# Loading stored sums of w_out in the later batches instead of adding them again on VectorE

## The chip, the cores and the metric

The kernel runs on one core of one Trainium2 chip. The metric is the time of one execution on the device in microseconds (us); less is better. Below, PE or TensorE is the matmul engine, DVE or VectorE the vector engine, ACT or ScalarE the scalar engine, POOL or GpSimd the engine whose queue issues software DMAs, and SP the engine that here only issues DMAs.

## The reference

There are two parts in a row. The attention part has 4 batches, 8 heads, 768 positions and 64 columns a head. Each query and key gets a hash of 6 bits from the signs of its product with proj; scores between a query and a key of different hash are masked; softmax and the product with v follow. The result, reshaped to 3072 x 512, goes through an MLP:

```
h = x @ w_in                                   # 512 -> 2048
g = max(h, 0) + alpha * min(h, 0)
out = g @ w_out                                # 2048 -> 512
```

All is float32. The change is in the last product, g @ w_out. Since w_out is the same for all four batches, so is everything that is computed from w_out alone.

## The kernel before, in words

`fast_path` first runs the attention of all 16 pairs of heads (up to about 375 us), and rounds and regroups the weights on the way. The MLP follows, batch by batch (768 tokens each). Each batch has eight blocks of the first stage (`ff1`, called "1" in the list of blocks) and seven of the second (`ff2`, called "2").

Both stages use a Strassen-like scheme with seven products in place of eight, twice nested in the second stage. The outer seven products of the second stage are the seven blocks n = 0 to 6, in the order `ORDER = (1, 2, 5, 6, 3, 7, 4)`; in the profile they carry the names z_1, z_2, z_5, z_6, z_3, z_7 and z_4. For each, `load_w2` has SP load one tile of 1 MB, `wl`, with the outer combination of quarters of w_out (from w_out_r, or, where it is a sum, from w_out_s). It has two buffers, and is issued two blocks ahead. The nested product then needs four quarters of `wl` and four sums of them, the tiles ws3, ws4, ws5 and ws6 (256 KB each), which `sum_w2` computes on VectorE: 3 = 21 + 2, 4 = 3 − 0, 5 = 0 − 21, 6 = 1 − 4. ws3 and ws4 have two buffers, ws5 and ws6 one (`bufs=1 + (m < 5)`). The same four sums for g are computed by `sum_g2` (tiles gs3 to gs6).

A product is an object of `Product`, whose seven matmul groups are the steps 1, 2, 5, 6, 3, 7 and 4 (22 is VectorE's part of step 2). Step 1 multiplies the first quarter of `wl`, step 2 the second, step 4 the third; step 5 uses ws3, step 6 ws4, step 3 ws6, and step 7 ws5. The loop over blocks starts step 1 of the next product ahead of step 4 of the current one, so TensorE's order within a block is 2, 5, 6, 3, 7, next 1, 4. Step 4 is the last to read the current `wl`, and its buffer is then free for the load two blocks on.

The instructions wrapped in `do(...)` keep their program order on their engine; all computing instructions are. Of the DMAs only some are (through `pinned`). The others, `wl` among them, are placed on their queue by a planner, which takes the instruction of the highest priority (earliest in the program) that can start by its own costs; a tile's buffer is given on when everything that reads it is done. On a queue the order is then fixed.

In batches 1 to 3 the first stage is nested as well (`unit`, `Inner`). The tags ws3 to ws6 are lent there to other tiles of the same size: two tiles `wp` of `load_inner` take ws3 and ws4, and two intermediate results take ws5 and ws6. The sums of block 0 are made at the end of `unit(b, 1)`. Finished outputs are transposed on VectorE by `turn_out` and stored by DMAs of 32 KB, 12 for each of four parts, on SP's queue and partly on GpSimd's.

A sum over w_in in the same manner is already kept: `sum_inner` computes it in batch 1 and stores it to w_n_s, and batches 2 and 3 load it.

Of the kernel before, what the change touches and what calls it, by code (L numbers as in the profile page):

```python
# [8 lines left out]
F32 = mybir.dt.float32  # L9
# [398 lines left out]
def fast_path(  # L408
# [12 lines left out]
    nc = tc.nc  # L421
    P = 128
    B, H, S, D = q.shape
    NB = proj.shape[1]
    NTOK, DM = out.shape
# [17 lines left out]
    do = tc.keep_in_program_order  # L443
    PE, DVE, ACT, POOL = nc.tensor, nc.vector, nc.scalar, nc.gpsimd

    const = ctx.enter_context(tc.tile_pool(name="const", bufs=1))
    dram = ctx.enter_context(tc.tile_pool(name="dram", bufs=1, space=bass.MemoryType.DRAM))
# [24 lines left out]
    NI = NF // 2  # L472
# [2 lines left out]
    w_out_r = dram.tile([4, P, NI, DM // 2], F32, name="w_out_r")  # L475
    w_out_s = dram.tile([4, P, NI, DM // 2], F32, name="w_out_s")
    x_s = dram.tile([B, NP, P, S], F32, name="x_s")
    w_n_s = dram.tile([2, 2, P, 4, 2 * P], F32, name="w_n_s")
    NW = NK * NF // 2
    wmax = const.tile([P, NW], F32, name="wmax")  # L480
# [405 lines left out]
    def sum_x(b, n, engine):  # L886

        to, a, c = ((3, 5, 0), (5, 2, 5), (4, 2, 3), (6, 4, 1))[n]
        if to != 5:
            x_m[b, to] = mid.tile([P, 2, CW], F32, name=f"x{b}_{to}", tag=f"x{to}", bufs=1)  # L890
        do(engine.tensor_tensor(x_m[b, to], x_m[b, a], x_m[b, c], op=ALU.subtract))
# [154 lines left out]
    def sum_inner(b, u, o):  # L1046

        if b != 1:
            return
        for m, x, op, y in ((3, 21, ALU.add, 2), (4, 3, ALU.subtract, 0), (5, 0, ALU.subtract, 21), (6, 1, ALU.subtract, 4)):  # L1050
            do(DVE.tensor_tensor(n_w[b, u, o, m], n_w[b, u, o, x], n_w[b, u, o, y], op=op))
            nc.gpsimd.dma_start(w_n_s[u, o, :, m - 3].rearrange("p (t f) -> p t f", t=2), n_w[b, u, o, m])

    def sum_inner_x(b, o):

        x = x_m[b, 3 * o]
        if o == 0:
            t = mid.tile([P, 4, HC], F32, name=f"xn{b}_0", tag="x", bufs=1)
        else:
            t = late[0].tile([P, 4, HC], F32, name=f"xn{b}_1", tag="gs5", bufs=1)  # L1060
        left, right = (x[:, :, c * HC : (c + 1) * HC] for c in range(2))
        do(DVE.tensor_tensor(t[:, :2], right, x[:, 0].rearrange("p (c w) -> p c w", c=2), op=ALU.subtract))
        do(DVE.tensor_tensor(t[:, 2], right[:, 1], t[:, 0], op=ALU.subtract))
        do(DVE.tensor_tensor(t[:, 3], left[:, 1], t[:, 2], op=ALU.subtract))
        n_x[b, o] = {0: left[:, 0], 1: left[:, 1], 2: right[:, 1], 3: t[:, 0], 4: t[:, 2], 5: t[:, 1], 6: t[:, 3]}
# [68 lines left out]
    def unit(b, u, before):  # L1134
# [31 lines left out]
        if u:  # L1166
            sum_w2(b, 0, 3, 4, 6, 5)
# [12 lines left out]
    w2, g2, m2, to_turn = {}, {}, {}, []  # L1180
# [25 lines left out]
    def sides_g(b, n):  # L1206
        t = g_m[b, SIDES[ORDER[n]][1]]
        for m, kh, ch in ((0, 0, 0), (1, 1, 0), (2, 1, 1), (12, 0, 1)):
            g2[b, n, m] = t[:, kh * HK : (kh + 1) * HK, ch * HC : (ch + 1) * HC]

    def sum_w2(b, n, *ms):

        if n < 7:
            for m in ms:
                x, op, y = {
                    3: (21, ALU.add, 2), 4: (3, ALU.subtract, 0), 5: (0, ALU.subtract, 21), 6: (1, ALU.subtract, 4),
                }[m]
                w2[b, n, m] = t = late[0].tile([P, HK, H2], F32, name=f"ws{b}_{n}_{m}", tag=f"ws{m}", bufs=1 + (m < 5))
                do(DVE.tensor_tensor(t, w2[b, n, x], w2[b, n, y], op=op))  # L1219

    def sum_g2(b, n, *ms):

        if n < 7:
            for m in ms:
                x, y = {3: (12, 0), 4: (2, 3), 5: (2, 12), 6: (1, 4)}[m]
                g2[b, n, m] = t = late[0].tile([P, HK, HC], F32, name=f"gs{b}_{n}_{m}", tag=f"gs{m}", bufs=1 + (m < 5))
                do(DVE.tensor_tensor(t, g2[b, n, x], g2[b, n, y], op=ALU.subtract))  # L1227
# [95 lines left out]
    def largest():  # L1323
        do(DVE.memset(col, 0.0))
        do(DVE.tensor_reduce(top[:, :2], mags, axis=mybir.AxisListType.X, op=ALU.max))
        do(DVE.tensor_reduce(top[:, 2:3], wmax, axis=mybir.AxisListType.X, op=ALU.max))
        do(DVE.tensor_reduce(top[:, 3:4], alpha, axis=mybir.AxisListType.X, op=ALU.max))

    def verdict():
        ps = two_banks("vd")[:4, 0, :P]  # L1330
        do(PE.transpose(ps, top, ident))
        do(DVE.tensor_reduce(col[:4, 0:1], ps, axis=mybir.AxisListType.X, op=ALU.max))
        do(DVE.transpose(row, col))
        do(DVE.tensor_tensor(row[0:1, 0:1], row[0:1, 0:1], row[0:1, 1:2], op=ALU.mult))

        do(DVE.tensor_scalar(row[0:1, 0:1], row[0:1, 0:1], SAFE, None, op0=ALU.is_le))
        do(DVE.tensor_scalar(row[0:1, 2:3], row[0:1, 2:3], HI_END, None, op0=ALU.is_lt))
        do(DVE.tensor_scalar(row[0:1, 3:4], row[0:1, 3:4], 1.0, None, op0=ALU.is_le))
        do(DVE.tensor_tensor(row[0:1, 0:1], row[0:1, 0:1], row[0:1, 2:3], op=ALU.mult))
        do(DVE.tensor_tensor(row[0:1, 0:1], row[0:1, 0:1], row[0:1, 3:4], op=ALU.mult))  # L1340
        do(DVE.tensor_scalar(flag, row[0:1, 0:1], -1.0, 1.0, op0=ALU.mult, op1=ALU.add))
# [130 lines left out]
    for j, (b, what, n) in enumerate(blocks):  # L1472
        n2 = n + 1 if what == "2" else 0 if n == NI - 1 else 7
        if n2 == 0:
            sides_g(b, 0)
            if b == 0:
                sum_w2(b, 0, 3, 4)
        if not j:
            now.step(6)
        elif not (b and what == "1"):  # L1480
            now.step(2)
        if j == 0:
            now.step(3)
            now.step(7)
            now.step(2)
        if what == "2" and n == 6 and b + 1 < B:
            sum_inner(b + 1, 0, 0)
        now.step(22)
        if (b, what, n) == (1, "2", 1):
            largest()  # L1490
        if what == "2" and b + 1 < B and 2 <= n < 6:
            if n == 3:
                sum_inner_x(b + 1, 0)
            else:
                sum_x(b + 1, {2: 0, 4: 1, 5: 2}[n], DVE)
        if b and what == "1" and n == 1:
            load_inner(b, 1)
        if b and what == "1" and n in (2, 3):
            sum_inner(b, 1, n - 2)
        if 0 < n2 < 7:  # L1500
            sides_g(b, n2)
            sum_w2(b, n2, 3, 4)
        if n2 < 7:
            sum_g2(b, n2, 3, 4)
        if j:
            if not (b and what == "1"):
                now.step(5)
            now.step(6)
            now.step(3)
            if n2 or b == 0:  # L1510
                sum_w2(b, n2, 6)
            if b and what == "1" and (n + 1) % 4:
                after = ff1(b, n + 1)
                after.step(1)
            now.step(7)
            if n2 or b == 0:
                sum_w2(b, n2, 5)
            sum_g2(b, n2, 5)
        if (b, what, n) == (1, "2", 3):
            verdict()  # L1520

        for n_out in [(), (0,), (1,), (2, 3), (4,), (5, 6), (7,)][j] if j < 7 else ():
            sum_out(n_out)
        for n_out in [(1,), (2, 3), (4,), (5, 6), (7,)][j] if j < 5 else ():
            load_out(n_out)
        if what == "1":
            load_w(b * NI + n + 3)

            if b and n in (2, 5):
                load_w2(b, n // 4)  # L1530
            if not b and n >= NI - 2:
                load_w2(b, n - NI + 2)
        else:
            load_w2(b, n + 2)
            if b + 1 < B:
                if n == 5:
                    load_inner(b + 1, 0)
                if n == 0:
                    load_x(b + 1)
        if j + 1 == len(blocks):  # L1540
            turn_last(0)
        elif what == "1" or n < 6:
            turn_out()
        before = now
        if j + 1 < len(blocks):
            b1, what1, n1 = blocks[j + 1]
            if b1 and what1 == "1" and n1 % 4 == 0:
                now = unit(b1, n1 // 4, before)
            elif b1 and what1 == "1":
                now = after  # L1550
                now.step(2)
                now.step(5)
                before.step(4)
            else:
                now = ff1(b1, n1) if what1 == "1" else ff2(b1, n1)
                now.step(1)
                before.step(4)
        else:
            before.step(4)
        if n2 < 7:  # L1560
            sum_g2(b, n2, 6)
# [29 lines left out]
```

## Time and profile before

| what | value |
|---|---|
| median of 3 runs | 866.09 us (865.49 to 866.65) |
| profiled execution, its own time | 865.96 us |
| its span, first to last instruction | 863.8 us |
| granted TensorE clock, mean | 0.998 of full |
| TensorE matmul busy | 851.8 us |
| VectorE busy | 751.6 us |
| ScalarE busy | 415.9 us |
| GpSimd busy | 150.1 us |
| the four sums `ws` (L1219) on VectorE | 38.4 + 19.4 + 19.2 us, 112 instructions |
| DMA, over the span | 147.97 MB, 28.24 of them on GpSimd's queue |

A row of the profile names the line of the kernel (L1219), the engine, the operation, and then the tile written and those read (`ws<-wl`), with the number of instructions; buffer numbers are left out of the names. In a group's row follow the busy time in us, the mean of one in ns, and after the bar the idle time of the engine just before them and who ended it. In a timeline row the first number is the start in us from the start of the span, the second the duration; merged rows carry a count (x8), and the time in square brackets is the wait before, with its releaser. A row of the waits reads: the waiting engine, tile and line, the releaser, the sum in us, the number, the longest. PEld is TensorE's weight load, which runs ahead of its matmul, so the same wait shows there a little longer.

The second stage of the four batches lies at about 385 to 452, 520 to 587, 655 to 722 and 789 to 855 us.

### The profile page before, as it was taken

Reading aid. Unit: us, or ns where it says so; the run is one execution under the profiler, and the core shown is the slowest. Engines: PE = TensorE matmul, PEld = TensorE weight load, DVE = VectorE, ACT = ScalarE, POOL = GpSimd, SP = SyncE. Lnnn points to the kernel's source line nnn. Section 1 sums busy time; section 2 is a strip of 40 time slices with the busy share of each in tenths; the row PEclk is TensorE's granted clock in tenths of the full one; section 3 lists DMA queues with packets and bytes.
Section 4 is the critical chain, followed back from the end, with each engine's and each line's share of the span. In section 5 each row is a group of like instructions: output and inputs, shape, how many; then the busy total and the mean of one; then the engine's idle time right before and its main releaser. Section 6 shows DMA issues by size and latency. Waiting matters only on the chain.

```text
span 863.8 us, 15130 instructions
## 1 busy us (share of the span) xinstructions
PE 851.8 (99%) x5602; PEld 591.1 (68%) x5602; DVE 751.6 (87%) x1210; ACT 415.9 (48%) x778; POOL 150.1 (17%) x313
## 2 busy tenths in 40 slices
PE   9999999999999999999999999999999999999996
PEld 4444444444445445569996769998668999677996
DVE  6999999999999977889996979996769997769985
ACT  7777888878788833231115541114452114453111
POOL 1322423333334310210015100003000001200001
PEclk9999999999999999999999999999999999999999
DMA  8956879879698436775344734333845334830342
GB/s 203 191 130 132 205 178 240 167 205 243 131 252 208 145 126 234 245 288 215 128 141 139 276 134 170 120 144 97 315 140 174 143 109 130 297 135 0 104 159 60
DMA packets 174659, 147.97 MB, mean 171 GB/s; under 512 B 120832, under 2 KB 155824, under 8 KB 170992
## 3 DMA queue, kind: packets, MB, share of 16 engines
q1 hardware_dynamic: 159776, 117.35, 46.7%
q0 software_dynamic: 11792, 28.24, 10.8%
q10 hardware_dynamic: 3008, 1.33, 0.6%
q8 instruction: 46, 0.75, 0.4%
q14 instruction: 37, 0.30, 0.1%
HBM read 115.35 MB, written 30.41 MB: 169 GB/s over the span
## 4 chain that ended last, share of the span: by engine, by line


## 5 line engine op out<-in xcount | busy, mean ns | idle before, releaser
L790 ACT ACTIVATE pt<-sc 128x768 f32<-128x768 f32 x192 | 153.9, 813 | 3.1 <-PE sc L787 2.8
L787 PE MATMUL sc<-qT,kT 64*128 64x384 f32 x768 | 155.2, 482 | 0.0
L820 PE MATMUL av<-pt,vn 128*32 128x385 f32 (+1 forms) x1536 | 127.0, 485 | 0.0
L820 PEld LDWEIGHTS av<-pt,vn 128*32 128x32 f32 x1536 | 50.3, 109 | 73.8 <-issue 68.8
L787 PEld LDWEIGHTS sc<-qT,kT 64*128 64x128 f32 x768 | 68.9, 187 | 37.0 <-issue 36.9
L1281 POOL DMA_DIRECT2D out_dram<-o x52 | 28.3, 552 | 349.6 <-DVE o L1274 348.8
L983 DVE TENSOR_TENSOR g<-g,g 128x384 f32<-128x384 f32 (+1 forms) x92 | 63.5, 711 | 1.6
L787 PE MATMUL sc<-qb,kb 64*128 64x384 bf16 x384 | 63.9, 323 | 0.5 <-ACT pt L790 0.3
L979 DVE SCALAR_TENSOR_TENSOR g<-h,alpha 128x384 f32<-128x384 f32 x63 | 37.8, 612 | 20.7 <-ACT h L972 20.7
L1227 DVE TENSOR_TENSOR gs<-g,gs 128x768 f32<-128x768 f32 x56 | 53.2, 951 | 1.0
L1227 DVE TENSOR_TENSOR gs<-g 128x768 f32<-128x768 f32 x56 | 53.2, 950 | 0.0
L1219 DVE TENSOR_TENSOR ws<-wl 128x512 f32<-128x512 f32 x56 | 38.4, 685 | 11.3 <-DMA wl<-w_out_s 9.7
L787 PEld LDWEIGHTS <-kb 64*128 64x128 bf16 x384 | 20.2, 94 | 33.9 <-issue 11.6
L607 ACT ACTIVATE wr<-raw 128x512 int32<-128x512 uint32 x32 | 22.1, 692 | 30.3 <-DVE wso L651 15.3
L748 POOL DMA_DIRECT2D qb<-hr x60 | 30.0, 507 | 26.4 <-ACT hr L743 26.4
L798 DVE TENSOR_TENSOR accp<-pt,pt 128x1536 f32<-128x1536 f32 x16 | 28.1, 1756 | 7.3 <-ACT pt L790 7.3
L803 DVE TENSOR_TENSOR accd<-accd,pt 128x1536 f32<-128x1536 f32 x16 | 28.1, 1758 | 1.7
L809 DVE TENSOR_TENSOR accd<-accd,accp 128x1536 f32<-128x1536 f32 x16 | 28.1, 1758 | 0.6
L806 DVE TENSOR_TENSOR accp<-accp,pt 128x1536 f32<-128x1536 f32 x16 | 28.0, 1752 | 0.0
L802 DVE TENSOR_TENSOR accd<-pt,pt 128x1536 f32<-128x1536 f32 x16 | 28.0, 1751 | 0.0
L1431 ACT ACTIVATE qT<-qT 128x768 f32<-128x768 f32 x15 | 12.7, 844 | 25.4 <-DMA kb<-hr 20.8
L1239 DVE TENSOR_TENSOR m<-m,m 128x768 f32<-128x768 f32 x24 | 22.7, 946 | 0.3
(448 smaller groups left out, 1861.0 us busy)
## 6 DMA issues: line engine op xcount, KB each, us to landing
wi<-w_in_s SPq DMA_DIRECT2D x32, 896.0 KB
wl<-w_out_s SPq DMA_DIRECT2D x16, 1024.0 KB
wl<-w_out_r SPq DMA_DIRECT2D x12, 1024.0 KB
raw<-in_moe_w_in_dram POOLq DMA_DIRECT2D x15, 512.0 KB, 4.9
raw<-in_moe_w_out_dram POOLq DMA_DIRECT2D x14, 512.0 KB, 4.6
w_in_s<-wsi SPq DMA_DIRECT2D x16, 448.0 KB
qn<-in_q_dram SPq DMA_DIRECT2D x64, 96.0 KB
vn<-in_v_dram SPq DMA_DIRECT2D x16, 384.0 KB
```

What stands on the lines that cost most here:

```text
L748: queue.dma_start(bits[name, pi][D * s : D * s + 2 * NB, half * CW : (half + 1) * CW], raw[c : c + 2 * NB],)
L787: do(PE.matmul(sc[:, s, :CW], what["k", pi][r, ks], what["q", pi][r, qs], start=first, stop=not first,))
L790: do(ACT.activation(pts[kc][:, g, :, :CW], sc[:, :, :CW], AF.Exp, scale=SCALE / DOWN))
L798: do(DVE.tensor_tensor(accp[pi], p(0), p(1), op=ALU.add))
L803: do(DVE.tensor_tensor(accd[pi], accd[pi], p(5), op=ALU.add))
L809: do(DVE.tensor_tensor(accd[pi], accd[pi], accp[pi], op=ALU.add))
L820: do(PE.matmul(av[pi][D * s + t : D * s + t + 32, g, :w], nat["v", pi][:, s, kc * D + t : kc * D + t + 32], pts[kc][:, g, s, :w], start=(k ...
L979: do(DVE.scalar_tensor_tensor(new_g(b, m)[:, i], h, al, h, op0=ALU.mult, op1=ALU.max))
L983: do(DVE.tensor_tensor(new_g(b, to)[:, at], g_m[b, x][:, at], g_m[b, y][:, at], op=ALU.subtract))
L1219: do(DVE.tensor_tensor(t, w2[b, n, x], w2[b, n, y], op=op))
L1227: do(DVE.tensor_tensor(t, g2[b, n, x], g2[b, n, y], op=ALU.subtract))
L1281: pinned(b + 1 < B and queue is nc.sync, queue.dma_start(out_v[b, ch * CH + c].rearrange("(w r) d -> r w d", r=32)[:, :, cols], src[32 * a ...
```

## The change

A tensor w_f_s in device memory is added, with a place for each of the seven products and four sums. In batch 0 the sums are computed on VectorE as before, and each is also stored to w_f_s by a DMA on GpSimd's queue. In batches 1 to 3 `sum_w2` issues a load of 256 KB on GpSimd's queue into the same tile, and VectorE adds nothing. The order in which the sums appear in the program changes for these batches too: all four of the next product are asked for at once, in the order 3, 4, 6, 5, where the first two were before, and not spread over the block. Neither stores nor loads are pinned. Buffers, products and all other loads stay as they are.

```diff
+    w_f_s = dram.tile([7, 4, P, NI // 2, DM // 4], F32, name="w_f_s")
...
                 w2[b, n, m] = t = late[0].tile([P, HK, H2], F32, name=f"ws{b}_{n}_{m}", tag=f"ws{m}", bufs=1 + (m < 5))
-                do(DVE.tensor_tensor(t, w2[b, n, x], w2[b, n, y], op=op))
+                if b:
+                    nc.gpsimd.dma_start(t, w_f_s[n, m - 3])
+                else:
+                    do(DVE.tensor_tensor(t, w2[b, n, x], w2[b, n, y], op=op))
+                    nc.gpsimd.dma_start(w_f_s[n, m - 3], t)
...
         if 0 < n2 < 7:
             sides_g(b, n2)
-            sum_w2(b, n2, 3, 4)
+            sum_w2(b, n2, *((3, 4, 6, 5) if b else (3, 4)))
...
             now.step(3)
-            if n2 or b == 0:
+            if b == 0:
                 sum_w2(b, n2, 6)
...
             now.step(7)
-            if n2 or b == 0:
+            if b == 0:
                 sum_w2(b, n2, 5)
             sum_g2(b, n2, 5)
```

## The prediction

> **What bounds the kernel now.** I read the page's first section, then TensorE's timeline in the last batch, then TensorE's waits from 380 us on (the change acts only after that), then the SP queue with VectorE's waits, then DMA shares by stretch.
>
> ```profile
> span 863.8 us, 15130 instructions
> PE 851.8 (99%) x5602; PEld 591.1 (68%) x5602; DVE 751.6 (87%) x1210; ACT 415.9 (48%) x778; POOL 150.1 (17%) x313
> ```
>
> TensorE looks full and VectorE nearly so. Busy matmuls alone prove little, so I check the pace of the second MLP stage. A product is seven TensorE steps in the order 2, 5, 6, 3, 7, 1 of the next product, 4. The start times:
>
> ```profile
> 816.11 1.46 PE L921 MATMUL z_6a<-g,wl 128*128 128x192 f32 x8
> ...
> 826.02 1.58 PE L921 MATMUL z_3a<-g,wl 128*128 128x192 f32 x8 [0.64 <-DMA wl<-w_out_s]
> ...
> 835.23 1.46 PE L921 MATMUL z_7a<-g,wl 128*128 128x192 f32 x8
> ...
> 844.33 1.46 PE L921 MATMUL z_4a<-g,wl 128*128 128x192 f32 x8
> ```
>
> From 835.23 to 844.33 is 9.10 us: seven steps of 1.30 us, the pace at which steps follow each other without a wait. Only 816.11 to 826.02 is longer, 9.91 us, and its row names the releaser: a 1 MB load of wl. All waits of TensorE after 380 us:
>
> ```profile
> PE z_2c L921 <- DVE m L1248: 0.8, 1, 0.8
> PE z_3a L921 <- DMA wl<-w_out_s: 0.6, 1, 0.6
> PE nf L1084 <- DVE wp L1051: 0.4, 1, 0.4
> PE z_4c L921 <- DVE m L1248: 0.3, 1, 0.3
> PE z_7c L921 <- DVE m L1248: 0.2, 1, 0.2
> PE f_3c L921 <- ACT f_3c L999: 0.2, 1, 0.2
> ```
>
> That is 2.5 us in 480. VectorE ends only three of them in a second-stage product: z_2c (in the first batch, where the additions stay) and z_7c and z_4c of the second batch. So TensorE sets the time, and VectorE, though 87% busy, is nearly always in time.
>
> The next thing that could be late is wl. SP issues the third to fifth wl of the last batch, and VectorE's first additions wait for each landing:
>
> ```profile
> 800.66 18.57 SPq L1187 DMA_DIRECT2D wl<-w_out_s  x3
> 805.41 0.69 DVE L1219 TENSOR_TENSOR ws<-wl 128x512 f32<-128x512 f32 x1 [0.28 <-DMA wl<-w_out_s]
> 814.50 0.69 DVE L1219 TENSOR_TENSOR ws<-wl 128x512 f32<-128x512 f32 x1 [1.20 <-DMA wl<-w_out_s]
> 826.00 0.69 DVE L1219 TENSOR_TENSOR ws<-wl 128x512 f32<-128x512 f32 x1 [3.56 <-DMA wl<-w_out_s]
> ```
>
> A wl is issued when step 4 frees its buffer (800.66, one 9.1 us later, the third at 818.9) and lands 4.7, 4.7 and 7.1 us after. TensorE wants it five steps after issue, at 6.5 us less the weight load that goes ahead: about 6.3 us. The usual margin is thus 1.6 us, but landings scatter: in the third batch one takes 5.2 us (667.10 to 672.29), in the second 6.2 (541.5 to 547.71), just in time. Last, the DMA engines in the quiet part of two products (start and end, us in the stretch, then the engines; the DMA share is the last but one):
>
> ```profile
> 805.90:809.80 3.90, 3.90 (x26) 3.90 (x26) 3.83 (x8) 0.64 (x2) 0.00 (x0) 1.00 0.00 0
> 815.00:818.90 3.90, 3.90 (x26) 3.90 (x26) 3.83 (x8) 0.64 (x2) 0.00 (x0) 1.00 0.00 0
> ```
>
> Share 0.00: once wl is in, the engines are empty until the next. In the 5.2 us before each, the shares are 0.56 and 0.54 of 2.6 us, so 1 MB costs 2.9 us of all sixteen engines and 256 KB costs 0.72 us (estimate from these).
>
> **The Trainium skill.** "Perfetto Trace Analysis", Identifying the Most-Contended Engine, says matmul busy time is a poor measure of headroom; hence the 9.10 us pace above. "DMA: Bandwidth & Descriptors", Issuing engines are not separate DMA queues, says queues of SP and GpSimd share the same sixteen engines: the new traffic can collide with wl although its queue differs. The trace before has no GpSimd traffic beside wl to show it. "SBUF — State Buffer", Who interferes with whom, says VectorE's two-port copies starve GpSimd's descriptor writing, while tensor_tensor does not; nearly all of VectorE's work here is tensor_tensor, and GpSimd's stores at L1052 were issued in 540 to 564 ns beside a busy VectorE, which agrees.
>
> **The change, part by part.**
>
> Removed: VectorE's four additions in each of 21 products (batches 1 to 3).
>
> ```profile
> L1219 DVE TENSOR_TENSOR ws<-wl 128x512 f32<-128x512 f32 x56 | 38.4, 685 | 11.3 <-DMA wl<-w_out_s 9.7 <-DMA wl<-w_out_r 1.4
> L1219 DVE TENSOR_TENSOR ws<-ws,wl 128x512 f32<-128x512 f32 x28 | 19.4, 692 | 1.0
> L1219 DVE TENSOR_TENSOR ws<-wl,ws 128x512 f32<-128x512 f32 x28 | 19.2, 684 | 0.1
> ```
>
> 84 of 112, 77.0 × 3/4 = 57.8 us of VectorE, 2.75 us a product, and the waits for wl ahead of them. On the path it is worth only the z_7c and z_4c waits, 0.5 and 0.6 us on the weight-load row: **−1.1 us**. The other products already run at 9.10. The first-batch 0.8 stays, as do nf and f_3c. z_3a waits for the transfer itself, which VectorE doesn't speed.
>
> Added, batch 0: 28 stores of 256 KB from GpSimd. Issue is 0.54 us (L1052's 128 KB) to 0.76 us (L1204's 512 KB) each; GpSimd is otherwise idle there, and nothing but w_n_s and output stores of the next stage queues behind. ws5 and ws6 have one buffer, so VectorE's next write now waits for the store to have read the last one; it has 9.1 us, a store lands in 2.7 (128 KB) to 7.2 us (512 KB, median). The cost is in the engines: VectorE ends the last two additions at about the moment the next wl is issued (batch 0: 415.03 and 415.90 against 415.95), so two stores, 1.4 us, share wl's window. Margin 1.6 us: TensorE hardly waits, but VectorE's next additions start later in a batch where it has 4% to spare. Bounds 0 to 3 us over five products; I take **+0.6**.
>
> Added, batches 1 to 3: 84 loads of 256 KB, four a product. Landing, between 128 KB (2.7 us) and 512 KB (4.6 to 4.9): 3.4 us, estimate. ws3 and ws4 have two buffers, so a load can run a product ahead. ws6 and ws5 have one: it is free after step 3 (or 7) and wanted at the same step one product later, 9.1 − 1.3 = 7.8 us. 7.8 − 3.4 leaves 4.4 us, so the new wait of TensorE on GpSimd's queue costs **0**. What hides it is that gap; it is gone only if a load takes over twice the estimate. If GpSimd holds at a buffer, only later ws loads or, at the start of the next batch, output stores stand behind, and nobody waits for those soon.
>
> Collision with wl: counted from wl's issue, buffers come free at 2.6 us (ws3), 3.9 (ws4), 5.2 (ws6) and 6.5 (ws5). Data follow over a microsecond later, so wl (done at 4.7) meets only the head of the ws3 load: at most 0.72 us against a usual margin of 1.6; where wl itself is slow, as in the 6.2 us case, that shows. Should GpSimd's queue instead run ws5, ws3, ws4 in a row, they fall between 6.5 us and the next wl. So regular products stay at 9.10. The exception is the product in which SP also sends 12 output stores (in the last batch from 821.4 us, 6.8 us long): there wl took 7.1 us and TensorE already waits, and the next wl is issued late behind them. Faster VectorE brings those stores 1 to 2 us forward, next to wl(4)'s issue, so perhaps one 0.55 us store gets ahead of it. Each of these can add 0.3 us, up to 1.3 in the worst (two ws loads wholly in front): bounds 0 to 1.3 for each of three batches, taken **+0.4 each, +1.2**.
>
> SP's instructions are the same in number, and ScalarE's too. TensorE gets waits on DMA beside those on VectorE; two waits may need a separate wait instruction, bounds 0 to 84 × 0.05 us = 4.2 (a wait instruction on VectorE's queue took 21 to 50 ns). I take 0: it runs ahead of the matmuls.
>
> Sum: −1.1 + 0.6 + 1.2 = +0.7. Against the profiled execution, 865.96 us (span 863.8 and 2.2 around it), that is 866.7; its own time is 0.13 below the median of 866.09, so **866.8 us**.
>
> **Rivals.**
>
> *Faster.* All waits that VectorE or wl ends in batches 1 to 3 vanish: 0.5 + 0.6 + 0.9 (z_3a on the weight-load row) = 2.0, and the stores in batch 0 cost nothing: 864.1. For it: VectorE drops to about 80%. Against: the 0.9 belongs to a transfer whose competition grows. Nothing more can be won, since all else is at matmul pace. Chance of passing the bound: 0.06.
>
> *Slower: wl is late.* Four loads double the traffic, from 1 MB to 2 MB in 9.1 us (share 0.33 to 0.65). If ws data fall in front of wl, each 256 KB moves it 0.72 us; from three loads in front (2.2 us) the 1.6 us margin is gone, from two where it lands at 5.2, and TensorE waits every product. At 0.5 us in 12 of the 15 products of three batches that load a wl, minus the 1.1, and 0.6 from the stores: 866.1 + 5.5 = 871.6; if only the products with output stores suffer, by 1.3 each, 869.5. For it: 7.1 us with output stores beside it. Against: buffers come free just after wl's data. Chance of over 0.2% slower: 0.41.
>
> *It doesn't do what it says:* GpSimd's loads are placed so late that TensorE waits for ws5 or ws6. That needs 7.8 us from free buffer to landing; L1204's slowest landed in 8.8 us, so it is thinkable for a few products, about 1 us each; it lies within the slower case.
>
> **How the numbers follow.** A measurement of this kernel tells about 0.2%, 1.7 us, from no change. My sum of +0.7 lies within it: chance 0.53. Faster by over 0.2% 0.06, slower 0.41. The range goes from 864.9 (the VectorE waits gone at no cost) to 870.5 (the milder slower cases); some 0.08 is left out below and 0.12 above.
>
> **What would show it.** VectorE busy 694 us, GpSimd's groups gain 28 stores and 84 loads (29 MB more in the software queue). Products of batches 1 to 3 still 9.10 us apart; z_4c and z_7c without waits on VectorE. Wrong if TensorE's waits name ws loads, if wl's landing after issue passes 6.3 us in regular products, or if SP's order around the 12 output stores differs and TensorE waits at z_3a or z_7a in every batch.

## The result, and the profile after

The changed kernel took 870.46 us (median of five runs, 869.72 to 873.14), the kernel before beside it 865.49 us (863.42 to 866.65). The ratio is 1.0064, with a 95% interval of 1.0042 to 1.0085: **slower by some 5.5 us** by the ratio, 5.0 by the medians. The forecast was 866.8 us, with no measurable difference as the likeliest case. The profiled execution took 870.30 us, span 868.4.

The page's first lines, and TensorE's waits from 380 us on:

```profile
span 868.4 us, 15362 instructions
PE 854.2 (98%) x5602; PEld 592.6 (68%) x5602; DVE 703.0 (81%) x1126; ACT 415.6 (48%) x778; POOL 210.2 (24%) x425
```

```profile
PE z_2a L922 <- DMA wl<-w_out_r: 3.3, 1, 3.3
PE z_7a L922 <- DMA wl<-w_out_s: 1.1, 1, 1.1
PE nf L1085 <- DVE wp L1052: 0.5, 1, 0.5
PE nc L1085 <- DVE wn L1052: 0.2, 1, 0.2
PE f_3c L922 <- ACT f_3c L1000: 0.2, 1, 0.2
```

VectorE lost 48.6 us of work (751.6 to 703.0; the forecast was 694), as was meant, and none of that is in the time. The VectorE waits at z_7c and z_4c in the second batch are gone, but a new wait of 3.3 us has appeared in the first batch, where nothing was taken away. No row names ws or GpSimd: no wait of TensorE ends with one of the 84 new loads.

First the part that went as planned. The pace in the last batch, the queue of SP around its output stores, and one of the stretches that were empty before:

```profile
820.73 1.46 PE L922 MATMUL z_6a<-g,wl 128*128 128x192 f32 x8
829.83 1.46 PE L922 MATMUL z_3a<-g,wl 128*128 128x192 f32 x8
840.18 1.57 PE L922 MATMUL z_7a<-g,wl 128*128 128x192 f32 x8 [1.08 <-DMA wl<-w_out_s]
849.39 1.46 PE L922 MATMUL z_4a<-g,wl 128*128 128x192 f32 x8
```

```profile
823.54 0.34 SPq L1286 DMA_DIRECT2D out_dram<-o  x1
823.97 0.38 SPq L1188 DMA_DIRECT2D wl<-w_out_s  x1
824.40 6.80 SPq L1286 DMA_DIRECT2D out_dram<-o  x11
832.62 0.34 SPq L1188 DMA_DIRECT2D wl<-w_out_s  x1
```

```profile
810.00:814.00 4.00, 4.00 (x27) 4.00 (x26) 1.58 (x3) 0.64 (x2) 1.10 (x3) 1.00 0.66 191
```

From 820.73 to 829.83 is 9.10 us: the regular pace holds with ws loads beside it. The DMA share in the once empty stretch is 0.66, and VectorE is busy for 1.58 of 4.00 us. One output store did get ahead of a wl (823.54), but that wl is z_3's, and z_3 starts in time. The late product is now z_7, 1.08 us, in place of z_3, 0.64. Its wl was issued at 832.62, right behind two ws loads:

```profile
831.57 1.07 POOL L1221 DMA_DIRECT2D ws<-w_f_s  x2 [3.34 <-PE z_3a L922]
```

Four more ws loads (835.49 to 839.39) were issued before it landed, some 7.6 us after its issue. Which of all these made it late was not tested. How VectorE's row and the new groups look:

```profile
L1223 DVE TENSOR_TENSOR ws<-wl 128x512 f32<-128x512 f32 x14 | 9.6, 688 | 8.0 <-DMA wl<-w_out_s 4.7 <-DMA wl<-w_out_r 3.4
L1221 POOL DMA_DIRECT2D ws<-w_f_s x84 | 45.2, 539 | 253.9 <-PE z_1c L922 88.2
L1224 POOL DMA_DIRECT2D w_f_s<-ws x28 | 15.2, 541 | 55.5 <-DVE ws L1223 41.0
...
ws<-w_f_s POOLq DMA_DIRECT2D x84, 256.0 KB, 3.4
w_f_s<-ws POOLq DMA_DIRECT2D x28, 256.0 KB, 4.3
```

A load lands 3.4 us after issue (the estimate was 3.4), a store 4.3. The first row is the one to stop at: the additions that remain, all in batch 0, now wait 8.0 us for wl. In the kernel before, VectorE waited 0.9 us for wl between 385 and 455 us.

Now that place. First the kernel before, then the kernel after, from the timeline; the column after the start is the duration, and wl is the 1 MB that z_2 needs:

```profile
388.51 0.32 SPq L1187 DMA_DIRECT2D wl<-w_out_r  x1
...
393.73 1.46 PE L921 MATMUL z_2a<-g,wl 128*128 128x192 f32 x8
```

```profile
383.61 0.55 POOL L1224 DMA_DIRECT2D w_f_s<-ws  x1 [2.58 <-DVE ws L1223]
384.34 0.55 POOL L1224 DMA_DIRECT2D w_f_s<-ws  x1 [0.17 <-issue]
388.45 0.54 POOL L1224 DMA_DIRECT2D w_f_s<-ws  x1 [3.56 <-DVE ws L1223]
389.19 0.32 SPq L1188 DMA_DIRECT2D wl<-w_out_r  x1
390.17 0.54 POOL L1224 DMA_DIRECT2D w_f_s<-ws  x1 [1.19 <-DVE ws L1223]
...
397.92 2.74 PE L922 MATMUL z_2a<-g,wl 128*128 128x192 f32 x8 [3.34 <-DMA wl<-w_out_r]
400.45 2.02 PE L922 MATMUL z_1a<-gs,wl 128*128 128x192 f32 x8
402.31 1.46 PE L922 MATMUL z_2b<-g,wl 128*128 128x192 f32 x8
```

Before, z_2 starts without a wait 5.2 us after wl's issue (388.51 to 393.73). That is less than the 6.3 us of a regular product, because this wl is issued late already: it takes a buffer that `wo`, a tile with the same tag, has held, and SP waits 8.0 us for the store of `wo` to be done:

```profile
379.60 0.75 POOL L1204 DMA_DIRECT2D w_out_s<-wo  x1 [6.57 <-DVE wo L1203]
```

After, wl is there only 8.7 us after issue (389.19 to 397.92). z_1's four stores stand around it: ws3's and ws4's five us ahead, ws6's just ahead and ws5's just behind. The stretch from 390 to 394 us, whose last three columns are granted TensorE clock, DMA share and GB/s, before and then after:

```profile
390.00:394.00 4.00, 4.00 (x26) 4.00 (x26) 3.93 (x7) 0.65 (x3) 0.00 (x0) 1.00 0.90 361
```

```profile
390.00:394.00 4.00, 4.00 (x27) 4.00 (x26) 3.93 (x7) 0.64 (x2) 0.54 (x1) 1.00 0.92 284
...
398.00:402.00 4.00, 4.00 (x15) 4.00 (x16) 3.93 (x7) 0.32 (x1) 1.08 (x2) 0.57 0.68 278
```

The engines were at 0.90 already; SP also loads 2 x 384 KB of x and 896 KB of wi behind this wl. There was no room, and with the stores the same share moves less, 284 in place of 361 GB/s. The last row shows a second price: after the wait the granted clock is 0.57. The 16 matmuls from 397.92 to 402.31 take 4.39 us in place of 2.60 (two steps of 1.30), so 1.8 us more. Wait and slow clock together are 5.1 us at this one place.

A smaller loss lies at the end of batch 0. From z_4's first matmul to the second na step of the next unit TensorE needs 16.61 us (445.30 to 461.91), before it needed 15.58 (440.45 to 456.03): 1.0 us, in pieces of 0.1 to 0.4 that VectorE ends. So +5.1 and +1.0 there and +0.4 at z_7a against z_3a; back come z_2c (0.9 us) and the second batch's two waits (1.1). That is +4.5, and the spans differ by 868.4 − 863.8 = 4.6. The sum leaves out two shifts that lie where the change does nothing and nearly cancel: TensorE comes to z_1 0.7 us later (388.53 to 389.22 for its step 5), and what follows its last step is 0.4 us shorter.

### The profile page after: what moved, and what is told of

Read it like the earlier page. It is cut to its first block, busy times and chain, and to the rows that moved or that the text cites. A ratio compares the mean times of both kernels' runs of the same rounds, so it can differ in the third digit from the quotient of the medians.

```text
span 868.4 us, 15362 instructions
## 1 busy us (share of the span) xinstructions
PE 854.2 (98%) x5602; PEld 592.6 (68%) x5602; DVE 703.0 (81%) x1126; ACT 415.6 (48%) x778; POOL 210.2 (24%) x425
## 4 chain that ended last, share of the span: by engine, by line
## 5 line engine op out<-in xcount | busy, mean ns | idle before, releaser
L1221 POOL DMA_DIRECT2D ws<-w_f_s x84 | 45.2, 539 | 253.9 <-PE z_1c L922 88.2
L1224 POOL DMA_DIRECT2D w_f_s<-ws x28 | 15.2, 541 | 55.5 <-DVE ws L1223 41.0
```

The source lines that it names most:

```text
L1221: nc.gpsimd.dma_start(t, w_f_s[n, m - 3])
```

## The experiments

"Wait" is always TensorE's unless another engine is named. The profiles are of one execution each; several of these kernels scatter by 4 us and more, so medians and intervals carry the verdicts and the traces the mechanism.

### Stores alone, loads alone

Only stores: all batches add on VectorE as before, and batch 0 stores as well.

```diff
-                if b:
-                    nc.gpsimd.dma_start(t, w_f_s[n, m - 3])
-                else:
-                    do(DVE.tensor_tensor(t, w2[b, n, x], w2[b, n, y], op=op))
+                do(DVE.tensor_tensor(t, w2[b, n, x], w2[b, n, y], op=op))
+                if b == 0:
                     nc.gpsimd.dma_start(w_f_s[n, m - 3], t)
```

> Batch 0 stores its sums as in the change, and nobody loads them: batches 1 to 3 add on VectorE as before. If the stores of batch 0 cost the time (theory A: they delay the 1 MB load of wl for z_2), this is 5 to 6 us slower than before, about 871, with TensorE waiting over 3 us at z_2a for wl<-w_out_r. If the loads of the later batches cost it (theory B, the prediction's slower rival), this is within 0.7 us of before.

Measured: 870.02 us, ratio 1.0064 [1.0049, 1.0079]. Its two largest waits:

```profile
PE z_5a L922 <- DMA wl<-w_out_s: 1.8, 1, 1.8
PE z_2a L922 <- DMA wl<-w_out_r: 0.9, 1, 0.9
```

The stores cost the whole loss. Which product is late is not fixed: in this execution (868.83 us) z_2 waits less and the next, z_5, more, and the clock doesn't fall.

Only loads: batches 1 to 3 load 256 KB of w_in_s, which are not the sums, into each ws tile, and nothing is stored.

```diff
                 if b:
-                    nc.gpsimd.dma_start(t, w_f_s[n, m - 3])
+                    nc.gpsimd.dma_start(t.rearrange("p n f -> p (n f)"), w_in_s[n, :, m - 3 : m - 1].rearrange("p a k f -> p (a k f)"))
                 else:
                     do(DVE.tensor_tensor(t, w2[b, n, x], w2[b, n, y], op=op))
-                    nc.gpsimd.dma_start(w_f_s[n, m - 3], t)
```

> Batches 1 to 3 load 256 KB tiles on GpSimd's queue as in the change, but from w_in_s, and batch 0 stores nothing; the values loaded are not the sums. Theory A: 0.5 to 1 us faster than before, about 864.8, with no wait of TensorE at z_7c and z_4c of batch 1. Theory B: about as slow as the change, 870.

Measured: 863.48 us, ratio 0.9986 [0.9976, 0.9996], 1.2 us faster than before. Waits of TensorE from 380 us on, all of them:

```profile
PE nf L1085 <- DVE wp L1052: 0.4, 1, 0.4
PE f_3c L922 <- ACT f_3c L1000: 0.2, 1, 0.2
```

So loads and relief of VectorE together are worth 1.2 us (0.3 to 2.1), and no cost of the 84 loads shows. That the loads bring the loss has fallen. How much of the 1.2 us is the relief stays open: z_2c of the first batch and z_3a of the last, which it doesn't touch, have no wait in this trace either.

### Which stores

A batch later: batches 0 and 1 add, batch 1 stores, batches 2 and 3 load (`if b > 1:` load; store `if b:`).

> The stores move from batch 0 to batch 1; batches 0 and 1 add on VectorE, batches 2 and 3 load. In batch 1 the wl for z_2 is loaded long ahead. Theory A: the 3.5 us wait at z_2a and the slow clock after it are gone; within 1 us of before, 865 to 866.5. Theory B: two thirds of the loss stay, about 869.

Measured: 864.73 us, ratio 0.9998 [0.9990, 1.0006]. The same 28 stores cost far less one batch later. Whether they are free there is open: the waits on VectorE that loads were to remove lie in batch 1, where this kernel still adds. Its profiled execution, 868.34 us, is the longest of 13, with a wait for wl of 1.2 us at z_7a in batch 2.

Without z_1's: its four sums are neither stored nor loaded (`if b and n:` load; store `if n:`).

> As the change, but the four sums of the first product, z_1, are neither stored nor loaded; VectorE adds them in every batch. Theory A in its narrow form (the four stores just ahead of and beside the wl load for z_2 are the cost): the wait at z_2a goes, about 4 us less than the change, near 866. If the stores as a whole cost the time, product by product, six sevenths of the loss stay, about 869.7.

Measured: 865.40 us, ratio 1.0009 [1.0000, 1.0017]. Leaving four stores out takes away most of the loss.

Only z_1's: these four alone are stored and loaded.

> Only the four sums of z_1 (the first product) are stored in batch 0 and loaded later; the other 24 sums are added on VectorE in every batch, as in the kernel before. Theory 'z_1's stores' (their 1 MB, issued by GpSimd just before and after the load of wl for z_2, shares the DMA engines with that wl, the x loads and w_out_s's store, so that wl lands some 3 us too late and TensorE's clock falls to half for a while after the wait): four stores alone bring nearly the whole loss, 4 to 5 us over the kernel before, about 869.3 us (868.3 to 870.3), with waits of TensorE for wl in z_2, z_5 or both. Rival 'all stores' (the loss comes from 28 stores, of which no four matter alone): 4/28 of 5, about 865.6 us (865.0 to 866.2).

Measured: 865.86 us, ratio 1.0025 [1.001, 1.004]. The time itself lies in the rival's range, but the kernel before beside it took 864.00 us: some 2 us more, between the rival's 0.7 and the theory's 4 to 5. It is scattered: eight executions took 863.3 to 866.0 us, five 867.7 to 870.1. The profiled execution (869.02 us) is one of the long ones and shows what the change shows: z_2a waits 2.8 us for wl, and the clock from 398 to 402 us is 0.57. So four stores are enough to make z_2's wl late, but not in every execution.

z_1's and z_2's eight (`n < 2` in the conditions for load and store):

> The eight sums of the first two products, z_1 and z_2, are stored in batch 0 and loaded later; the other 20 are added on VectorE in every batch. Theory 'crowded start' (in the first two products of batch 0 the engines are nearly full anyway with w_out_s, x and wi; there z_1's stores make z_2's wl late in part of the executions, and where they do not, z_2's stores make z_5's wl late): eight stores bring nearly the whole loss, 868.4 us (867.2 to 869.6), against 864.4 of the kernel before; waits of TensorE for wl at z_2a or z_5a of 1.5 us or more, no such wait later in batch 0. Rival 'costs add up' (four stores cost 2 us, 24 cost 1 us): 866.3 us (865.5 to 867).

Measured: 867.79 us, ratio 1.0032 [1.0021, 1.0044], within the range of "crowded start", with waits of 1.2 us at z_2a and 2.5 at z_5a. But its complement, the twenty stores from z_5 on, did not come out:

> The complement: the 20 sums of the third to seventh product are stored in batch 0 and loaded in batches 1 to 3; z_1's and z_2's sums are added on VectorE in every batch. Theory 'crowded start': the stores are free, and 5/7 of VectorE's relief remains: 0.7 to 1.2 us under the kernel before, 863.4 us (862.8 to 864.2). Rival 'costs add up' (20 of the 24 stores whose cost was about 1.9 us against loads alone): 864.9 us (864.4 to 865.6), no faster than the kernel before.

Measured: 866.65 us, ratio 1.0023 [1.0014, 1.0032]: above both forecasts, and slower than before, where the theory had it faster. These stores are not free either. Crowding at the start of batch 0 is only part of the cause.

Later for z_1 and z_2: as that one, with their eight sums stored in batch 1 and loaded in batches 2 and 3.

> A candidate for beating both kernels: the 20 sums from the third product on are stored in batch 0 and loaded in batches 1 to 3; z_1's and z_2's eight sums are stored in batch 1 instead, and loaded in batches 2 and 3. Theory 'crowded start': in batch 1 the start of the second stage has no w_out_s traffic beside it, so the stores are free there: 863.3 us (862.6 to 864.2), faster than the kernel before by about 1. Rival 'costs add up': 865.3 us (864.8 to 866.0). Third possibility: batch 1's stores of z_1 stand beside its 12 output stores and make wl late there: 865.5 us, with a wait for wl in batch 1.

Measured: 866.85 us, ratio 1.0026 [1.0016, 1.0035]: above all three forecasts, and no better kernel. The wait for wl in batch 1 that the third one named is in its trace, 1.0 us at z_6a.

Smaller: z_1's four stores with a quarter of their bytes (`w_f_s[n, m - 3, :, :1]` from `t[:, :1]`), on top of the kernel without them.

> As the kernel without the stores of z_1, but z_1's four stores are issued after all, with a quarter of their bytes (64 KB each, nobody loads them). Theory 'bytes' (the stores take the engines' time from wl): 4 x 0.18 us of engine time in place of 4 x 0.72, no wait of over 1 us at z_2a: as without them, 865.2 us (864.6 to 866.0). Rival 'the store itself' (any store of GpSimd's beside wl delays it, whatever its size): as the whole change, 869.5 us (868.5 to 870.5).

Measured: 866.07 us, ratio 1.0013 [1.0003, 1.0023], a touch above the range for "bytes" and far from 869.5. What costs here is bytes, not the fact of a store. z_2a still waits 1.0 us in the profile, so 64 KB are not shown to be free.

### Where in the product

ws3 and ws4 are stored in the gap after a wl has landed, ws6 and ws5 just as the next wl is issued. Four kernels split the sums so. First ws3 and ws4 of the last six products (`n and m < 5` in the conditions):

> Only ws3 and ws4 of the six products after z_1 are stored and loaded; ws5 and ws6 and all of z_1's sums are added on VectorE. ws3 and ws4 are finished well before the next wl is issued, so by the theory 'stores in wl's window' (the prediction's own: the last two sums of a product are stored at the moment the next wl is issued) nothing collides and half of VectorE's relief remains: 864.2 us (863.6 to 864.7), faster than the kernel before by 0.4 to 1. Rival 'any store costs the same' (what is left without z_1's stores, 1.9 us against loads alone, is spread over 24 stores): 0.95 lost and 0.7 won, 865.0 us (864.7 to 865.5).

Measured: 863.83 us, ratio 0.9996 [0.9988, 1.0004]. Then ws5 and ws6 of the same products (`n and m > 4`):

> The counterpart: only ws5 and ws6 of the six products after z_1 are stored and loaded; ws3, ws4 and z_1's sums are added on VectorE. Theory 'stores in wl's window': these twelve carry the whole remaining cost of 1.9 us, against half of the relief (0.7): 866.0 us (865.5 to 866.6), slower than the kernel before. Rival 'any store costs the same': as its counterpart, 865.0 us (864.7 to 865.5).

Measured: 865.20 us, ratio 1.0009 [1.0001, 1.0018]. The first lies in the theory's range, the second in the rival's. Then the two halves with z_1's sums too, `m < 5` and `m > 4`:

> Only ws3 and ws4, of all seven products, are stored in batch 0 and loaded later; ws5 and ws6 are added on VectorE in every batch. Theory 'beside wl': these fourteen stores end before the next wl is issued, z_1's two at 383.6 us too, five before it; half of the relief remains: 864.0 us (863.4 to 864.9), no slower than the kernel before. Rival 'any store': half of the loss, 867.0 us (866.3 to 867.8).

Measured: 863.86 us, ratio 0.9996 [0.9988, 1.0004].

> The counterpart: only ws5 and ws6, of all seven products. Theory 'beside wl': these fourteen stores carry nearly the whole loss: 868.3 us (867.3 to 869.6), with waits of TensorE for wl at z_2a or z_5a in batch 0. Rival 'any store': half of it, 867.0 us (866.3 to 867.8).

Measured: 865.31 us, ratio 1.0011 [1.0001, 1.0022]. In both pairs the stores of ws3 and ws4 cost nothing that shows, and those of ws5 and ws6 cost about 1 us. But the halves come nowhere near the whole: −0.0004 and +0.0011 against +0.0064. Neither "beside wl" (which wanted most of the loss in the second half) nor "any store" (half of it in each) has the size right. The cost of the stores is not a sum over stores. The traces of the last two show part of the reason: neither half of z_1's stores makes z_2a more than 0.3 us late. A mixture without z_1's sums, ws3 and ws4 stored in batch 0, ws6 and ws5 in batch 1, was no better:

> A candidate for beating both kernels: no sum of z_1 is stored; ws3 and ws4 of the other six products are stored in batch 0 and loaded in batches 1 to 3; ws6 and ws5 are added in batches 0 and 1, stored in batch 1, and loaded in batches 2 and 3. Theory 'stores in wl's window': the stores of ws6 and ws5 now meet batch 1's quieter traffic; 864.0 us (863.4 to 864.7). Rival 'any store costs the same': 1.9 lost, 1.2 won, 865.5 us (865.0 to 866.0).

Measured: 865.45 us, ratio 1.0017 [1.0008, 1.0025].

### Moving the late stores

In batch 0 GpSimd first copies one column of the next product's wl and only then stores ws6 and ws5, so that they start when that wl has landed. Every store and load of the change is kept.

```diff
+            if b == 0 and n and 3 in ms:
+                do(POOL.tensor_copy(late_sum, w2[b, n, 0][:, 0, :1]))
+                while held:
+                    do(nc.gpsimd.dma_start(*held.pop(0)))
...
-                    nc.gpsimd.dma_start(w_f_s[n, m - 3], t)
+                    if m < 5 or n == 6:
+                        do(nc.gpsimd.dma_start(w_f_s[n, m - 3], t))
+                    else:
+                        held.append((w_f_s[n, m - 3], t))
```

> As the change, but in batch 0 GpSimd stores ws6 and ws5 of a product only when the next product's wl has landed (it first copies one column of that wl to a scratch tile); ws3 and ws4 are stored at once as before. Same 28 stores, same 84 loads. Theory 'beside wl' (a store costs only while it shares the engines with a wl in flight): the loss goes and VectorE's relief stays, 863.2 us (862.4 to 864.1), faster than the kernel before by about 1, with no wait of TensorE for wl over 0.5 us in batch 0 and VectorE's waits for wl there under 2 us in sum. Rival 'any store': as the change, 869.3 us (868 to 870.5).

Its control copies from the current product's wl (`w2[b, n - 1, 0]`), which has long landed, so that nothing is delayed:

> The control of the delayed stores: the same code and the same order on GpSimd's queue, but the copied column is one of the current product's wl, which landed a product ago, so ws6 and ws5 are stored as soon as they are computed. Theory 'beside wl': as the change, 869.3 us (868 to 870.5). Rival 'order of GpSimd's queue' (what helps is the fixed order, not the delay): 863 to 864.5 us.

Measured: delayed 868.60 us, ratio 1.0052 [1.0030, 1.0074], scattered from 866.1 to 872.5; control 868.78 us, ratio 1.0047 [1.0029, 1.0065]. The control did as expected. The delayed one, expected at 863.2 us, took as long as the control. The start of z_2 in the control's trace:

```profile
397.82 2.05 PE L922 MATMUL z_2a<-g,wl 128*128 128x192 f32 x8 [3.20 <-DMA wl<-w_out_r]
```

The same with the stores delayed: GpSimd's copy, z_2's start, and VectorE's next write to ws6:

```profile
393.82 0.56 POOL L1218 COPY late_sum<-wl 128x1 f32<-128x1 f32 x1 [8.85 <-DMA wl<-w_out_r]
394.56 1.46 PE L922 MATMUL z_2a<-g,wl 128*128 128x192 f32 x8
400.48 0.69 DVE L1229 TENSOR_TENSOR ws<-wl,ws 128x512 f32<-128x512 f32 x1 [2.43 <-DMA w_f_s<-ws]
```

Without ws6's and ws5's stores beside it, z_2's wl is in at 393.8, 4.9 us after its issue at 388.97, and z_2 starts with no wait. With them it took until 397.8. These are two executions; the other traces agree. Where an engine's wait shows its landing, this wl lands 5.0 us after issue with none of z_1's stores in batch 0 (the kernel with z_1 and z_2 a batch later), 6.0 with the four small ones, 6.1 with ws6 and ws5 alone, and 6.5 to 8.7 in the five traces with all four at full size. TensorE wants it four steps after z_1's step 5 begins, which is 4.7 to 6.6 us after issue over all twenty traces, since the store of `wo` ahead of it takes 7.5 to 9.5 us. So z_1's stores make this wl later by up to 3.7 us, and how much of that TensorE sees differs from trace to trace.

That alone is not the loss of time: the delayed store meets its single buffer, and VectorE waits 2.4 us to write the next ws6. Nor is that the rest of it: this execution (867.22 us) is among the shorter ones, with a span only 1.6 us over that of the kernel before, so most of what the median lost is in no trace.

### VectorE's slack

In batch 0 VectorE was busy for 43.54 of the 45 us from 400 to 445 before the change, 97%; in the stretch of batch 1 from 535 to 580 after it, 34.45, 77%. So what a late wl costs VectorE could be made up in batch 1 and hardly in batch 0. The last pair takes gs5 and gs6 off VectorE in batch 0, once in the kernel with the twenty stores from z_5 on, once in the kernel before:

```diff
+                if b == 0 and m > 4:
+                    g2[b, n, m] = g2[b, n, x]
+                    continue
```

> The kernel with stores and loads of the third to seventh product only, and in batch 0 VectorE leaves out two of the four sums of g for each product (gs5 and gs6; TensorE reads a quarter of g in their place, and the output is that of other numbers), 1.9 us a product. To be compared with the kernel before with the same two sums left out. Theory 'no slack in batch 0' (the stores make wl later, VectorE waits for it and cannot make it up): with slack the stores cost nothing and the loads' relief shows, 0.5 to 1.2 us under its partner, about 862.0 us (861.3 to 863.2). Rival 'late for TensorE itself': the same 2.2 us over its partner as without the slack, about 865.0 us (864.3 to 866.0).

> The partner: the kernel before, with gs5 and gs6 of batch 0 left out in the same way (the output is that of other numbers). Both theories: VectorE's waits in batch 0 and at the next batch's start go (0.9 at z_2c, 0.4 at nf), 863.0 us (862.2 to 863.8), about 1 under the kernel before.

Measured: with stores 864.52 us, ratio 1.0004 [0.9996, 1.0012]; the partner 863.68 us, ratio 0.9989 [0.9981, 0.9997]. The difference is 0.8 us by the medians and 0.0015 by the ratios, against 0.0023 without slack. The intervals of the two overlap, so the times don't decide: 864.52 us lies in the rival's range, but 0.8 us over the partner is far from the rival's 2.2. The forecast gain of 0.5 to 1.2 could not come: the partner's trace no longer has the z_7c and z_4c waits that the loads would remove. What changed in the traces shows in TensorE's waits from 380 to 462 us. Without slack:

```profile
PE z_2c L922 <- DVE m L1254: 0.8, 1, 0.8
PE nf L1085 <- DVE wp L1052: 0.5, 1, 0.5
PE nc L1085 <- DVE wn L1052: 0.2, 1, 0.2
PE z_7a L922 <- DMA wl<-w_out_s: 0.2, 1, 0.2
PE z_1a L922 <- DVE gs L1233: 0.2, 1, 0.2
```

With slack there is one, nf with 0.4 us. At the same time VectorE's own waits for wl are larger, 10.6 us in place of 3.0:

```profile
DVE ws L1223 <- DMA wl<-w_out_s: 10.6, 4, 3.2
```

That is slack being spent: VectorE has the time to wait. The stretch from z_4's first matmul to the second na step is 15.57 us with slack (439.95 to 455.52) and 16.61 without (441.65 to 458.26). The loss of 1.0 us at the end of batch 0, which the change has as well, is thus VectorE's missing slack, as far as one execution of each shows.

## Why the prediction was wrong

**What bounds the kernel: right.** TensorE's pace set the time in both kernels, and the empty DMA stretches in regular products were there to be used.

**Removed, −1.1: right in size.** The two waits are gone, and loads alone brought 1.2 us (0.3 to 2.1). That it was these two waits is not shown: the partner with slack adds in batch 1 and has no load, and its trace lacks them too.

**Added, batches 1 to 3, waits for GpSimd's queue at 0: right.** No wait names a ws load; landing was 3.4 us as estimated.

**Collision in the products with output stores, +1.2: too high.** Loads alone show no wait for wl at all. An output store did move ahead of z_3's wl, as was said, in the change and with loads alone, and z_3 didn't wait. In the changed kernel z_7a lost 1.1 us in one batch where z_3a had lost 0.6: 0.4 us once, not in three batches, and with two ws loads issued just ahead of its wl, the case that the term put last.

**Added, batch 0, +0.6 with bounds 0 to 3: the step that failed.** The runs put 5.5 us (4.2 to 6.8) in its place. The argument was that two stores, 1.4 us, share wl's window, against a margin of 1.6 us. Both numbers came from regular products of the last batch, where the engines are otherwise empty, and were carried to five products of batch 0. (The 415.03 and 415.90 beside them are when the two additions start, not when they end; they end 0.7 us later, which changes little.) For z_2 there is no such margin. TensorE wants its wl 5.2 us after issue and not 6.3, and the DMA share was 0.88 and 0.90 from 385 to 394 us before the change, with SP's loads of x and wi behind wl. The trace before had that row. What "The Trainium skill" says in "DMA: Bandwidth & Descriptors", Issuing engines are not separate DMA queues, was cited and holds; the trace now shows it (wl there 8.7 us after issue with the four stores around it, 4.9 with two of the four moved away).

The same step said that VectorE's additions would "start later in a batch where it has 4% to spare", and put no price of its own on it. In the traces the price was 1.0 us at the batch's end, which is gone with slack.

Third, no step had the clock. It was worth 1.8 us in the profiled execution.

**The rival *Slower: wl is late*** named the right victim, but by the ws loads in every product of batches 1 to 3. It was the stores, in the first products of batch 0. Its milder time, 869.5 us, was near 870.46 by another road; that, and the upper end of the range at 870.5, is luck. The rival that TensorE waits for ws loads did not occur.

**What stays open.** Four stores of z_1 cost 0.0025, the other 24 cost 0.0009, all together 0.0064; the two halves by position cost −0.0004 and 0.0011, each with its own relief in it. The traces offer a reason why it is no sum: there is a limit up to which a delay is absorbed (wl's margin, VectorE's few per cent, in some executions and not in others), and past it come a wait and the slow clock. For z_2 it is the 4.7 to 6.6 us after issue at which TensorE wants its wl; for the later products it was not measured. The delayed stores, too, cost 0.0052 with z_2's wl in time in the one execution that was traced. Why the twenty stores from z_5 on cost no less than 24 that include z_2's (1.0023 against 1.0009, with intervals that touch) was not settled. And no kernel that computes everything was shown to be faster than the one before; those that store only ws3 and ws4 equal it.

## What to carry to other kernels

A precomputed value is paid for where it is stored, in the batch that still does the work: look for the margin there, not in the batches that are relieved. Before a transfer is added, ask for the DMA share in the stretch of each product that it will meet, the first ones above all, and not in a regular product alone. And where an engine is 97% busy, a delay of its input is passed on; moving the delay behind a single buffer only moved the wait to VectorE here.

## What the hardware showed

A wait can cost TensorE more than its own length. After the waits of 3.3 us (the change), 3.2 (the control) and 2.8 (z_1's stores alone) the clock granted in the stretch from 398 to 402 us was 0.57, 0.60 and 0.57; after one of 2.5 us (z_1's and z_2's stores) it stayed at 1.00:

```profile
407.27 1.58 PE L922 MATMUL z_5a<-g,wl 128*128 128x192 f32 x8 [2.52 <-DMA wl<-w_out_s]
```

"TensorE: Matmul & The Clock Gate", Part 1: The HAM clock gate, in the Trainium skill, says that the clock falls to half after at least one idle window of about 3.4 us. Here a wait of 2.8 us, as the trace has it, was enough in one execution. In all three the clock fell only 0.2 to 1.1 us after TensorE had started again, and stayed at half for about 3.4 us, whatever the length of the wait. In the change, two steps took 4.39 us in place of 2.60.

Two transfers of 256 KB on the same queue differ by direction and place: the 84 loads landed 3.4 us after issue (median), the 28 stores of the crowded batch 4.3.
